# Gate logits of four query chunks in one PSUM bank, spread over the partitions through DRAM: a change to a kernel that mixes two attention blocks

## The chip, the cores and the metric

One core of one Trainium2 chip. The metric is the device time of one execution in microseconds (us). "Span" is the time from the first to the last instruction in a profiled execution; it is some 2 us (up to 3) shorter than the device time of the same run. Engines: PE multiplies, with PEld for its weight loads; ACT is ScalarE, DVE VectorE, POOL GpSimd; SP only issues transfers.

## The reference

Two blocks read 2048 rows of 512 columns and a gate mixes them, row by row:

```python
x = A_x                                                     # [1, 2048, 512] bf16
g = sigmoid((x * gate_w).sum(-1, keepdims=True))            # one number per row
a = softmax attention(x), 32 heads of width 16, then @ A_wo
b = linear attention(x) with phi(t) = t + 1 or exp(t), then @ B_wo
return g * a + (1 - g) * b
```

## The kernel before

The kernel holds a **planner**: tasks are generators that yield steps, each with an engine, an estimated duration and an instruction. The planner picks, time step by time step, what each engine does next, and writes one fixed order of instructions per engine. On the chip every engine runs its own list in order and waits on semaphores. A few dozen constants steer the choices.

The score units (128 keys x 512 queries of one head) have two ways to their exponential: in pairs on ACT, or one at a time on DVE by integer arithmetic on the bits of a bf16, with two shifted copies that DVE or POOL makes. A unit on DVE costs PE three products instead of one. 2048 units are shared out by the planner.

```python
    SWITCH = 100.0
    FILL = 0.7
    HOT = 32.85
    BACK = 980.186
    # ... some forty such constants
    PKR, MTR, PQR, PQS, FR = 0.404, 8.73, 13.55, 1.600, 0.0
    KR, KS, QR = 5.59, 1.48, 4.00

        # matmul on four column tiles of 32, all with the same moving operand
        def mmt(o, l, r, start=True, stop=True):
            def go():
                for j in range(4):
                    h = nc.tensor.matmul(o[32 * j:32 * j + 32], lhsT=l[:, 32 * j:32 * j + 32], rhs=r, start=start, stop=stop,
                                         skip_group_check=True)
                return h
            return go

        def t_v(t8, vb):
            # ... project V, then copy it out of PSUM on DVE:
            yield dv(607, lambda: nc.vector.tensor_copy(Vc[:, 0, vs, :, :, 0:16], src), [r_bank[b]], [r_V[vs]])
            yield ("FREE", b)
            for k in range(1, NTERM):       # two scaled copies of V on POOL, for the units on DVE
                yield po(690, lambda k=k: nc.gpsimd.tensor_scalar(Vc[:, k, vs].rearrange("p a b c -> p (a b c)"),
                                                                  Vc[:, 0, vs].rearrange("p a b c -> p (a b c)"), COEF[k], 1.0,
                                                                  op0=ALU.mult, op1=ALU.mult), [r_V[vs]], [r_V[vs]])

        def t_gate():                       # abridged: see the diff
            # weights copied to 4 x 128 columns on POOL; per chunk of 512 queries: 16 matmuls into a bank of its own,
            # one DVE transpose, one POOL copy of 16 columns; then exp, + 1, reciprocal, 1 - g, four loads of gnat

        def aout(r):                        # after a round of attention; gt is g, natural layout
            # ...
            gv = gt[:, qc, :].unsqueeze(1).to_broadcast([128, n, 16])
            yield dv(155 + 17 * n, lambda: nc.vector.reciprocal(rc, src[:, :, :, 16]), rT1, rr)
            yield po(230 + 25 * n, lambda: nc.gpsimd.tensor_tensor(rgc, rc, gv, ALU.mult), [*rr, r_gt], rrg)
```

The softmax here doesn't subtract the row's maximum and nothing guards it: scores larger than these inputs give would overflow.

## Time and profile before

| | before |
|---|---|
| device time, median of three | 675.63 us |
| span of the profiled run | 674.2 us |
| ACT busy / idle | 658.3 / 15.9 us |
| exponentials of 128x1024 on ACT | 695 (1390 units) |
| units on DVE | 658 |
| ACT idle at the start and end | 9.7 us before 40 us, 6.05 us after 660 us |

In the profile's lines of groups, the columns are line, engine, operation, destination and source, shapes and count, then busy us and mean ns, then the engine's idle time just before them and what ended it. In a time line they are start, length, instruction, and idle time before it in square brackets. The prediction below shows the lines of before.

### The profile page before, as it was taken

The numbers are of one execution on the slowest core, as the hardware profiler recorded it, in microseconds if no ns is written. First come the engines' busy times: TensorE is split into PE (matmuls) and PEld (weight loads), VectorE is DVE, ScalarE is ACT, GpSimd is POOL, SyncE is SP. The second block draws the span as 40 slices with busy tenths as digits, with TensorE's granted clock in tenths as the row PEclk, the third lists the DMA queues.
The fourth block names the chain that finished last, engine by engine and source line by source line (L and its number), as shares of the span: only waits on it lengthen the run. The fifth ranks groups of instructions, "written<-read, shape, count | busy, mean of one in ns | idle before, by whom it ended". The sixth has DMA issues, their size and how long they took to land.

```text
span 674.2 us, 23975 instructions
## 1 busy us (share of the span) xinstructions
PE 660.7 (98%) x9813; PEld 202.2 (30%) x9839; DVE 603.4 (89%) x1053; ACT 658.3 (98%) x735; POOL 559.4 (83%) x617
## 2 busy tenths in 40 slices
PE   8999999999999999999999999999999999999998
PEld 3322323232322232323333322232232332222222
DVE  6999989988888889989999888999899998899985
ACT  6899999999999999999999999999999999999996
POOL 3789888888978888888888888878888989887881
PEclk9999999999999999999999999999999999999999
DMA  6420001200000000000001000001010020000001
GB/s 133 135 84 11 6 1 36 70 10 2 3 10 1 10 2 3 10 2 11 4 2 45 30 10 1 8 12 30 6 34 10 18 42 25 24 19 11 26 17 33
DMA packets 28155, 15.96 MB, mean 24 GB/s; under 512 B 19984, under 2 KB 27024, under 8 KB 28048
## 3 DMA queue, kind: packets, MB, share of 16 engines
q1 hardware_dynamic: 26704, 13.92, 8.2%
q8 instruction: 79, 1.29, 0.8%
q10 hardware_dynamic: 1344, 0.52, 0.3%
q14 instruction: 28, 0.23, 0.1%
HBM read 6.69 MB, written 2.10 MB: 13 GB/s over the span
## 4 chain that ended last, share of the span: by engine, by line
PE 50%; ACT 31%; issue 12%; SPq 2%; DVE 2%; POOL 1%; DMA 1%; ACTq 0%; DVEq 0%; POOLq 0%
PE ps L377 39%; ACT P L778 30%; PE ps L383 10%; SPq L354 2%; DVE Z L692 1%; ACT eb L1083 1%; POOL Z L746 1%; DMA gwc<-in_gate_w_dram 1%; DVE Z L756 0%; POOL Vc L995 0%; SPq L358 0%; ACTq L1495 0%; DVE OAT L1059 0%; DVE wA L1176 0%; DVE T L1031 0%
## 5 line engine op out<-in xcount | busy, mean ns | idle before, releaser
L778 ACT ACTIVATE P<-ps 128x1024 bf16<-128x1024 f32 x695 | 645.5, 1117 | 3.9 <-PE ps L377 3.7
L746 POOL TENSOR_TENSOR Z<-Z,mcon 128x512 int32<-128x512 int32 x471 | 488.0, 1061 | 64.4 <-DVE Z L692 50.4
L692 DVE TENSOR_SCALAR Z<-ps 128x512 int16<-128x512 f32 x658 | 440.4, 683 | 57.2 <-PE ps L377 50.9
L377 PE MATMUL ps<-Qz,KT 32*128 32x512 bf16 x2048 | 271.8, 384 | 3.9 <-ACT P L778 1.7
L377 PE MATMUL ps<-Z,Vc 128*17 128x512 bf16 x1974 | 272.5, 382 | 0.5 <-DVE Z L756 0.3
L377 PE MATMUL ps<-P,Vc 128*17 128x512 bf16 x1390 | 245.0, 383 | 1.0 <-POOL Vc L995 1.0
L377 PEld LDWEIGHTS ps<-Qz,KT 32*128 32x128 bf16 x2048 | 67.8, 91 | 262.7 <-ACT P L778 228.7
L377 PEld LDWEIGHTS ps<-Z,Vc 128*17 128x17 bf16 x1974 | 60.9, 88 | 69.1 <-issue 44.2
L756 DVE TENSOR_SCALAR Z<-Z 128x1024 int16<-128x1024 int16 x187 | 77.3, 433 | 0.0
L377 PEld LDWEIGHTS ps<-P,Vc 128*17 128x17 bf16 x1390 | 55.5, 88 | 60.1 <-issue 46.0
L377 PE MATMUL ps<-warm 128*32 128x512 bf16 (+16 forms) x529 | 55.9, 326 | 4.7 <-issue 2.4
L383 PE MATMUL ps<-xT,wA 128*32 128x512 bf16 (+1 forms) x528 | 43.4, 376 | 0.0
L1084 POOL TENSOR_SCALAR eb<-eb 128x512 f32<-128x512 f32 x32 | 21.0, 656 | 18.7 <-DVE Z L756 10.1
L995 POOL TENSOR_SCALAR Vc<-Vc 128x576 bf16<-128x576 bf16 x32 | 21.7, 679 | 6.0 <-DVE Vc L992 2.3
L377 PEld LDWEIGHTS ps<-warm 128*32 128x32 bf16 (+1 forms) x555 | 19.4, 96 | 18.4 <-issue 10.3
L383 PE MATMUL ps<-wA,OAT 128*32 128x512 bf16 x256 | 23.0, 382 | 0.1
L1071 POOL TENSOR_TENSOR T<-T,rg 128x256 bf16<-128x256 f32 x31 | 19.6, 631 | 4.1 <-PE ps L377 1.0
L1083 ACT ACTIVATE eb<-ps 128x512 f32<-128x512 f32 x32 | 22.7, 709 | 0.0
L383 PE MATMUL ps<-xT,wB 128*32 128x512 bf16 x256 | 22.3, 382 | 0.0
L383 PE MATMUL ps<-wA,xnat 128*32 128x512 bf16 x256 | 22.3, 381 | 0.0
L1035 DVE STREAM_TRANSPOSE T<-ps 128x512 f32<-128x512 f32 x31 | 21.9, 706 | 0.1
L1085 DVE SCALAR_TENSOR_TENSOR phiK<-ps,eb 128x512 bf16<-128x512 f32 x32 | 21.7, 678 | 0.2 <-POOL eb L1084 0.2
(81 smaller groups left out, 276.1 us busy)
## 6 DMA issues: line engine op xcount, KB each, us to landing
Qz<-QT SPq DMA_DIRECT2D x120, 16.0 KB, 1.8
wA<-in_A_wqkv_dram SPq DMA_DIRECT2D x4, 384.0 KB, 4.3
wB<-in_B_wqkv_dram SPq DMA_DIRECT2D x4, 384.0 KB, 3.0
xnat<-in_A_x_dram SPq DMA_DIRECT2D x3, 512.0 KB, 3.8
out_dram<-outt SPq DMA_DIRECT2D x12, 128.0 KB, 1.7
wA<-in_A_wo_dram SPq DMA_DIRECT2D x1, 512.0 KB, 4.6
wA<-in_B_wo_dram SPq DMA_DIRECT2D x1, 512.0 KB, 6.5
out_dram<-wA SPq DMA_DIRECT2D x4, 128.0 KB, 1.7
```

The lines of the kernel that those rows point to most:

```text
L377: return lambda: nc.tensor.matmul(o, lhsT=l, rhs=r, start=start, stop=stop, skip_group_check=sg)
L383: h = nc.tensor.matmul(o[32 * j:32 * j + 32], lhsT=l[:, 32 * j:32 * j + 32], rhs=r, start=start, stop=stop, skip_group_check=True)
L692: return C(DV, OPP, 533 * n + 74, lambda: nc.vector.tensor_scalar(o, i, ZB, 0.0, op0=ALU.add, op1=ALU.max), [r_bank[b] for b in bks], r_Z[ ...
L746: return C(PO, 400, 70 + 484 * n, lambda: nc.gpsimd.tensor_tensor(Z[:, z, 0:512 * n].bitcast(I32), Z[:, z0, 0:512 * n].bitcast(I32), mcon[ ...
L756: return C(DV, 450 if hot else 300, 69 + 134 * n, lambda: nc.vector.tensor_scalar(Z[:, z, 0:512 * n], Z[:, z0, 0:512 * n], float(m), None, ...
L778: return C(AC, 500, 427 * n + 49, lambda: nc.scalar.activation(P[:, slot, 0:512 * n], bank(b0, n), ACT.Exp, scale=ESC), [r_bank[b0 + k] fo ...
L995: yield po(690, lambda k=k: nc.gpsimd.tensor_scalar(Vc[:, k, vs].rearrange("p a b c -> p (a b c)"), Vc[:, 0, vs].rearrange("p a b c -> p ( ...
L1035: yield dv(607, lambda: nc.vector.transpose(T1[:, a, :], bank(7)), [r_bank[7]], [r_T1[a]])
L1071: yield po(640, lambda k=k: nc.gpsimd.tensor_tensor(dst_[:, k], src[:, k, :, 0:16], rgc[:, k].unsqueeze(2).to_broadcast([128, 16, 16]), AL ...
L1083: yield ac(480, lambda: nc.scalar.activation(eb[:, i, :], bank(b), ACT.Exp), [r_bank[b]], [r_eb[i]])
L1084: yield po(640, lambda: nc.gpsimd.tensor_scalar(eb[:, i, :], eb[:, i, :], 1.0 + 1e-6, 0.0, op0=ALU.min, op1=ALU.max), [r_eb[i]], [r_eb[i]])
L1085: yield dv(607, lambda: nc.vector.scalar_tensor_tensor(dst_ap, bank(b), 1e-6, eb[:, i, :], op0=ALU.max, op1=ALU.add), [r_bank[b], r_eb[i]] ...
```

## The change

The four chunks' logits go into one bank, one chunk per column tile, with 32 weight columns instead of 128. One transpose then gives all logits, but with the chunks in different partition quarters. The sigmoid is taken on 16 columns. To have every quarter see all chunks, the result is stored to a DRAM buffer of 8 KB and loaded four times, once per quarter, into gt, which holds g for the first block; gnat, loaded from it by way of POOL, holds 1 - g for the second. The diff also sets twelve of the planner's constants anew.

```diff
-    HOT = 32.85
-    BACK = 980.186
+    HOT = 45.668
+    BACK = 977.283
     ... and PLATE, SLK, AGE, PEP, HOLD, BIAS, TTOL, MTR, PQS, KR
         def t_gate():
-            yield po(900, lambda: nc.gpsimd.tensor_copy(gwr, gwc[:].unsqueeze(2).to_broadcast([128, NCC, 128])), [r_gw], [r_gwr])
-            yield ("WAIT", lambda: ("x", 0) in flags and phi_free[0])
-            phi_free[0] = False
-            for qc in range(NQC):
-                b = yield ("BANK",)
-                for h in range(2):
-                    yield pe_step(2, 512, [mmt(bank(b), gwr[:, cc, :], xT[:, cc, 512 * qc:512 * (qc + 1)], ...)
-                                           for cc in (2 * h, 2 * h + 1)], ...)
-                yield dv(607, lambda b=b: nc.vector.transpose(gl, bank(b)), [r_bank[b]], [r_gl, *r_outt])
-                yield ("FREE", b)
-                yield po(250, lambda qc=qc: nc.gpsimd.tensor_copy(ge[:, qc, :], gl.rearrange("p (a b) -> p a b", b=32)[:, :, 0]), ...)
-            ... exp, + 1, reciprocal, 1 - g on 64 columns; four loads of gnat
+            yield po(400, lambda: nc.gpsimd.tensor_copy(gwr, gwc[:].unsqueeze(2).to_broadcast([128, NCC, 32])), [r_gw], [r_gwr])
+            yield ("WAIT", lambda: all(("x", t) in flags for t in range(NQC)))
+            b = yield ("BANK",)
+            def g4(cc):
+                def go():
+                    for j in range(4):
+                        h = nc.tensor.matmul(bank(b)[32 * j:32 * j + 32], lhsT=gwr[:, cc, :], rhs=xT[:, cc, 512 * j:512 * (j + 1)], ...)
+                    return h
+                return go
+            for h in range(2):
+                yield pe_step(2, 512, [g4(2 * h), g4(2 * h + 1)], ...)
+            yield dv(607, lambda: nc.vector.transpose(gl, bank(b)), [r_bank[b]], [r_gl, *r_outt])
+            yield ("FREE", b)
+            ... exp on ACT, + 1 on POOL, reciprocal on DVE, 16 columns each
+            yield ("DMA", scr, ge[:, 0, :], semGN, 16, 2500.0, [r_ge], [r_scr], False, True)
+            for a in range(4):
+                yield ("DMA", gt[32 * a:32 * (a + 1), :, :], scr.rearrange("(q i) b -> i q b", q=NQC), semGT, 64, ...)
+            yield po(200, lambda: nc.gpsimd.tensor_scalar(gp[:], gt[:].rearrange("p q (c a) -> p a (q c)", a=4), -1.0, 1.0, ...),
+                     [r_gt], [r_gp])
+            ... four loads of gnat from gp
             yield ("FLAG", lambda: flags.add("gate"))
```

More of the change, by code (lines that the diff above doesn't have):

```diff
@@ L164, in bass_gated_mix__mha_block__linear_attn_block__prompt_kernel @@
     PMIN = 2
-    PLATE = -199.667
-    SLK = 88.975
+    PLATE = -168.321
+    SLK = 146.603
     DSL = 843.776
@@ L171, in bass_gated_mix__mha_block__linear_attn_block__prompt_kernel @@
     DENS = 0.743
-    AGE = 300.0
-    PEP = 148.771
+    AGE = 140.993
+    PEP = 147.128
     PVD = 216
@@ L176, in bass_gated_mix__mha_block__linear_attn_block__prompt_kernel @@
     MZD = 0.0
-    HOLD = 109.508
+    HOLD = 16.447
     NACT = 4
-    BIAS = 82.599
+    BIAS = 65.881
     KEYW = 7.061
@@ L182, in bass_gated_mix__mha_block__linear_attn_block__prompt_kernel @@
     DTOL = 186.116
-    TTOL = 37.928
-    PKR, MTR, PQR, PQS, FR = 0.404, 8.73, 13.55, 1.600, 0.0
-    KR, KS, QR = 5.59, 1.48, 4.00
+    TTOL = 64.585
+    PKR, MTR, PQR, PQS, FR = 0.404, 8.00, 13.55, 1.835, 0.0
+    KR, KS, QR = 6.02, 1.48, 4.00
     NB = 2
@@ L231, in bass_gated_mix__mha_block__linear_attn_block__prompt_kernel @@
         T2 = SB([128, 2, 512], BF16, "T2")
-        gwr = T2[:, 0, :].rearrange("p (c n) -> p c n", c=NCC)
+        gwr = T2[:, 0, 0:128].rearrange("p (c n) -> p c n", c=NCC)
         OAT = SB([128, NT8, S], BF16, "OAT")
@@ L242, in bass_gated_mix__mha_block__linear_attn_block__prompt_kernel @@
         gt = SB([128, NQC, 16], FP32, "gt")
-        ge = SB([128, NQC, 16], FP32, "ge")
+        ge = SB([128, 2, 16], FP32, "ge")
+        gp = SB([128, 4, 16], FP32, "gp")
+        scr = nc.dram_tensor("gate_rows", [128, 16], FP32).ap()
         gnat = SB([128, NKB], FP32, "gnat")
@@ L288, in bass_gated_mix__mha_block__linear_attn_block__prompt_kernel @@
         r_mcon = R("mcon")
-        r_gt, r_ge, r_gl, r_gnat = R("gt"), R("ge"), R("gl"), R("gnat")
+        r_gt, r_ge, r_gl, r_gp, r_gnat, r_scr = R("gt"), R("ge"), R("gl"), R("gp"), R("gnat"), R("scr")
         r_OBT = [R(f"OBT{i}") for i in range(NKB)]
@@ L399, in bass_gated_mix__mha_block__linear_attn_block__prompt_kernel @@
         semGN = SEM("s_gn")
+        semGP = SEM("s_gp")
+        semGT = SEM("s_gt")
         semOB = [SEM(f"s_ob{i}") for i in range(2)]
@@ L1000, in t_gate @@
         def t_gate():
-            yield po(900, lambda: nc.gpsimd.tensor_copy(gwr, gwc[:].unsqueeze(2).to_broadcast([128, NCC, 128])), [r_gw], [r_gwr])
-            yield ("WAIT", lambda: ("x", 0) in flags and phi_free[0])
-            phi_free[0] = False
-            for qc in range(NQC):
-                b = yield ("BANK",)
-                for h in range(2):
-                    yield pe_step(2, 512, [mmt(bank(b), gwr[:, cc, :], xT[:, cc, 512 * qc:512 * (qc + 1)], start=(cc == 0), stop=(cc == NCC - 1))
-                                           for cc in (2 * h, 2 * h + 1)], [r_xT[qc][h], r_gwr], [r_bank[b]])
-                yield dv(607, lambda b=b: nc.vector.transpose(gl, bank(b)), [r_bank[b]], [r_gl, *r_outt])
-                yield ("FREE", b)
-                yield po(250, lambda qc=qc: nc.gpsimd.tensor_copy(ge[:, qc, :], gl.rearrange("p (a b) -> p a b", b=32)[:, :, 0]),
-                         [r_gl, *r_outt], [r_ge])
@@ L1013, in t_gate @@
-            phi_free[0] = True
-            yield ac(300, lambda: nc.scalar.activation(gt[:], ge[:], ACT.Exp, scale=-1.0), [r_ge], [r_gt])
-            yield po(200, lambda: nc.gpsimd.tensor_scalar(ge[:], gt[:], 1.0, None, op0=ALU.add), [r_gt], [r_ge])
-            yield dv(650, lambda: nc.vector.reciprocal(gt[:], ge[:]), [r_ge], [r_gt])
-            gp = ge[:].rearrange("p q c -> p (q c)")
-            yield po(200, lambda: nc.gpsimd.tensor_scalar(gp.rearrange("p (a u) -> p a u", a=4), gt[:].rearrange("p q (c a) -> p a (q c)", a=4),
-                                                          -1.0, 1.0, op0=ALU.mult, op1=ALU.add), [r_gt], [r_ge])
@@ L1020, in t_gate @@
-            for a in range(4):
-                yield ("DMA", gnat[32 * a:32 * (a + 1), :], gp[32 * a:32 * (a + 1), 16 * a:16 * (a + 1)], semGN, 64, 2500.0, [r_ge], [r_gnat], False, a == 0)
+            yield po(400, lambda: nc.gpsimd.tensor_copy(gwr, gwc[:].unsqueeze(2).to_broadcast([128, NCC, 32])), [r_gw], [r_gwr])
[4 more added lines that the diff above has]
+                    for j in range(4):
+                        h = nc.tensor.matmul(bank(b)[32 * j:32 * j + 32], lhsT=gwr[:, cc, :], rhs=xT[:, cc, 512 * j:512 * (j + 1)],
+                                             start=(cc == 0), stop=(cc == NCC - 1), skip_group_check=True)
+                    return h
+                return go
@@ new lines, in t_gate @@
+            for h in range(2):
+                yield pe_step(2, 512, [g4(2 * h), g4(2 * h + 1)], [*[r_xT[t][h] for t in range(NQC)], r_gwr], [r_bank[b]])
+            yield dv(607, lambda: nc.vector.transpose(gl, bank(b)), [r_bank[b]], [r_gl, *r_outt])
+            yield ("FREE", b)
+            yield ac(230, lambda: nc.scalar.activation(ge[:, 0, :], gl.rearrange("p (a b) -> p a b", b=32)[:, :, 0], ACT.Exp, scale=-1.0),
+                     [r_gl, *r_outt], [r_ge])
+            yield po(150, lambda: nc.gpsimd.tensor_scalar(ge[:, 1, :], ge[:, 0, :], 1.0, None, op0=ALU.add), [r_ge], [r_ge])
@@ new lines, in t_gate @@
+            yield dv(170, lambda: nc.vector.reciprocal(ge[:, 0, :], ge[:, 1, :]), [r_ge], [r_ge])
+            yield ("DMA", scr, ge[:, 0, :], semGN, 16, 2500.0, [r_ge], [r_scr], False, True)
+            for a in range(4):
+                yield ("DMA", gt[32 * a:32 * (a + 1), :, :], scr.rearrange("(q i) b -> i q b", q=NQC), semGT, 64, 2800.0, [r_scr], [r_gt], False, a == 0)
+            yield po(200, lambda: nc.gpsimd.tensor_scalar(gp[:], gt[:].rearrange("p q (c a) -> p a (q c)", a=4), -1.0, 1.0, op0=ALU.mult, op1=ALU.add),
+                     [r_gt], [r_gp])
@@ L1022, in t_gate @@
+            for a in range(4):
+                yield ("DMA", gnat[32 * a:32 * (a + 1), :], gp[32 * a:32 * (a + 1), a, :], semGP, 64, 2500.0, [r_gp], [r_gnat], False, a == 0)
             yield ("FLAG", lambda: flags.add("gate"))
```

## The prediction

> **What bounds the kernel now.** I read the page's engine table first, then the chain that ended last, then the costliest groups, then the windows, then the waits of ACT, and last the time line around the one large hole that they showed.
>
> ```profile
> PE 660.7 (98%) x9813; PEld 202.2 (30%) x9839; DVE 603.4 (89%) x1053; ACT 658.3 (98%) x735; POOL 559.4 (83%) x617
> PE 50%; ACT 31%; issue 12%; SPq 2%; DVE 2%; POOL 1%; DMA 1%; ACTq 0%; DVEq 0%; POOLq 0%
> ...
> L778 ACT ACTIVATE P<-ps 128x1024 bf16<-128x1024 f32 x695 | 645.5, 1117 | 3.9 <-PE ps L377 3.7
> L746 POOL TENSOR_TENSOR Z<-Z,mcon 128x512 int32<-128x512 int32 x471 | 488.0, 1061 | 64.4 <-DVE Z L692 50.4
> L692 DVE TENSOR_SCALAR Z<-ps 128x512 int16<-128x512 f32 x658 | 440.4, 683 | 57.2 <-PE ps L377 50.9
> ...
> L756 DVE TENSOR_SCALAR Z<-Z 128x1024 int16<-128x1024 int16 x187 | 77.3, 433 | 0.0
> L377 PE MATMUL ps<-warm 128*32 128x512 bf16 (+16 forms) x529 | 55.9, 326 | 4.7 <-issue 2.4
> ```
>
> Two engines show 98%. PE's figure is flattered: 55.9 us of it are matmuls on the tile warm, which feed nothing and stand where PE would have waited. ACT's is real work, the exponentials of the softmax. The chain alternates between the two because every exponential waits for scores and every score pair waits for a free bank. So I ask where ACT itself is idle:
>
> ```profile
> 0.00:20.00 20.00, 18.05 (x268) 7.74 (x269) 14.28 (x26) 13.56 (x16) 9.44 (x32) 1.00 0.61 126
> 20.00:40.00 20.00, 18.86 (x377) 6.89 (x375) 17.97 (x31) 16.71 (x19) 16.02 (x20) 1.00 0.41 124
> 40.00:660.00 620.00, 612.70 (x9024) 183.84 (x9044) 563.92 (x979) 619.89 (x693) 533.01 (x567) 1.00 0.07 17
> 660.00:674.20 14.20, 11.04 (x161) 3.68 (x153) 7.19 (x20) 8.15 (x11) 0.96 (x1) 1.00 0.11 38
> ```
>
> The columns are stretch, length, then busy time of PE, PEld, DVE, ACT and POOL, clock, DMA share and GB/s. ACT is idle 6.4 us at the start, 3.3 us from 20 to 40, 0.1 us over the next 620 us, and 6.05 us at the end: 15.9 us, which with 658.3 busy makes the span of 674.2. Between 40 and 660 us the kernel is ACT's queue and nothing else. Only two things can shorten it: fewer exponentials on ACT, or smaller holes at the ends.
>
> The largest hole, 2.48 us, has a history that the time line tells, one engine after the other (ACT, POOL, PE):
>
> ```profile
> 21.54 1.02 ACT L778 ACTIVATE P<-ps 128x1024 bf16<-128x1024 f32 x1 [0.21 <-PE ps L377]
> 25.05 1.02 ACT L778 ACTIVATE P<-ps 128x1024 bf16<-128x1024 f32 x1 [2.48 <-PE ps L377]
> ...
> 20.00 1.15 POOL L746 TENSOR_TENSOR Z<-Z,mcon 128x512 int32<-128x512 int32 x1 [0.34 <-DVE Z L692]
> 22.38 0.61 POOL L1001 COPY T<-gwc 128x512 bf16<-128x512 bf16 x1 [1.23 <-DMA gwc<-in_gate_w_dram]
> 23.07 1.47 POOL L995 TENSOR_SCALAR Vc<-Vc 128x576 bf16<-128x576 bf16 x2
> ...
> 24.60 0.40 PE L377 MATMUL ps<-P,Vc 128*17 128x512 bf16 x4 [0.98 <-POOL Vc L995]
> ```
>
> POOL's queue is in order. The gate's copy of the weights (L1001) waits 1.23 us for its load, runs 0.61 us, and only then come the two scaled copies of V, for which PE's next product waits; behind that product stand the scores that ACT wants. So a piece of the gate is on the path once, at 22 us. The rest of it lies between 30.5 and 59 us, beside a busy ACT.
>
> **What the Trainium skill says.** "TensorEngine Tiling (Array Packing)", Key Properties: different tiles can load weights and multiply in parallel. The trace agrees: four gate matmuls on four column tiles take 0.39 us, eight 0.61, twelve 0.83, so 0.22 us for each further four. Four products of P and Vc, which stream four different operands, also take 0.40, so giving each tile its own query chunk should cost nothing. "DMA: Bandwidth & Descriptors", Anatomy of one DMA: a small DMA costs about 2 us fixed, mostly the receipt of the write, longest when the target is HBM, and semaphore waits happen on the issuing sequencer. The trace has 1.7 us for the 2 KB pieces of gnat and 1.8 for Qz; no run here yet shows a small store that is read back. "VectorE: DVE Perf Modes", The three transpose paths: the DVE transpose works on 32x32 blocks. That is why 32 equal columns of logits per chunk suffice, and the trace times one bank at 0.706 us.
>
> **The change, part by part.** PE: 64 matmuls, 16 rounds of four, become 16, four rounds; 12 x 0.22 = 2.6 us less. They can displace matmuls on warm, so alone this is worth about nothing. DVE: four transposes become one, 3 x 0.706 = 2.1 us less; the reciprocal shrinks from 64 to 16 columns, where the trace has 0.553 at 64, 0.334 at 32 and 0.204 at 8 columns, so about 0.25 (estimate), 0.3 less. Sum 2.4 us. POOL: four copies of 0.202 go (0.8); the weight copy falls from 512 to 128 columns, 0.61 to about 0.3 (estimate, from 0.20 for 16 columns and 0.30 for 64); the addition falls from 0.38 to about 0.2. Sum 1.3 us. ACT: the one exponential goes from 0.315 to about 0.25, under 0.1 us. Three other PSUM bank occupations of the gate go too.
>
> Added: one store of 8 KB and four loads of 8 KB through DRAM, in front of the four loads of gnat that stay. The four issues of gnat took 2.41 us; so issue and landing of the store about 0.6 + 2.0, of the loads 2.4 + 1.8, then POOL 0.3: the gate table gt is ready some 7 us after the reciprocal (estimate). gt is first needed by L1069, at 58.6 us. The one matmul step needs all of x, whose last transposing load was issued at 16.97 us and lands about 3 us later, so it can run by 25 to 35 us; with 2 us for transpose, exponential, addition and reciprocal gt is there by 45 us at the latest. Slack over 10 us: the round trip is hidden.
>
> What is on the path: the weight copy in front of V, 0.3 us shorter; the wait for its load stays unless the order changes. The freed DVE and POOL time is worth something only where the static schedule turns it into score units taken off ACT. There are 695 x 2 + 658 = 2048 units. A unit on DVE costs (440.4 + 77.3) / 658 = 0.79 us there plus 488.0 / 658 = 0.74 us of POOL; on ACT it costs 645.5 / 1390 = 0.46 us. DVE's 2.4 us buy three units, which is 1.4 us of ACT; POOL's 1.3 us and its idle 17% can follow. Sum: 0.3 + 1.4 + 0.1 = 1.8 us, if all is collected.
>
> The diff also retunes some fifteen constants of the scheduler that lays out the static order. They decide how eagerly DVE takes units, when POOL takes shifts and when the second block's projections begin. I cannot compute their effect; it reorders nearly every instruction. New values were presumably picked because they do well with the smaller gate, so I expect 0 to 4 us of gain, centred near 1. A stretch where ACT lost 0.1 us in 620 leaves them little but the share of units and the two ends.
>
> **Rivals.** (1) The wait moves. The SP queue is in order, and the store waits for the reciprocal, the loads for the store, the gnat loads for POOL. If the gate comes at 32 us, the eight Qz loads of the second pair, issued at 35.62 before, queue behind some 7 us. The first exponential was at 9.31 and a round of 64 units lasts about 620 / 2048 x 64 = 19 to 20 us, so those Qz are needed near 49 us; landing moves from about 43 to 50. For it: everything shares one queue. Against: the scheduler knows these waits and SP idles long otherwise. It would cost 1 to 2 us of ACT once: 674 to 676. (2) The hole at 22 us closes. With another order, V's copies would follow the shift that ended at 21.15, 1.9 us sooner than 23.07, and ACT would get most of 2.48 us back: with the 1.8 above some 671.5 to 672. For it: the new order is drawn afresh; against: the copy is still the gate's first step with the same release. (3) Nothing is collected: the 2.4 us of DVE become idle time, as 50.9 us of waiting for PE before L692 already are, and the time stays at 675 to 676. (4) The retuning finds a better split, say ten units more off ACT, 4.6 us: 669 to 671. DVE at 89% and POOL at 83% leave room, the matmuls on warm too.
>
> **Range and chances.** Direct effects -1.8 us if collected, taken at two thirds: -1.2; retuning -1; the hole at 22 us -0.7 as a weighted chance; queueing on SP +0.2. Together -2.7 us from 675.6, so 673.0. The three runs before spread 1.5 us, and a reordered schedule may move 2 to 3 us either way; the low side is wider because constants are usually kept when they help. Range 668.5 to 676.5. Two per cent is 13.5 us, nearly all of ACT's idle time, or 29 units; faster than that 0.03, slower 0.02, within 0.95.
>
> **What would show it.** In the changed profile: 16 matmuls on xT and the gate weights, one transpose, no copy to ge; ACT near 657 us with 692 to 694 exponentials, and D units 662 to 664; ACT idle under 0.5 us from 40 to 650; gt read by L1069's counterpart without a wait on a DMA. Rival 1 shows as PE or POOL waiting for a DMA of Qz or gt between 40 and 60 us; rival 2 as ACT's idle time from 20 to 40 us falling from 3.3 to about 1; rival 3 as 695 exponentials again; rival 4 as 690 or fewer. The prediction is wrong if the count of exponentials moves by more than five, or if either end of the kernel changes by more than 3 us.

## The result

673.93 us (median of four, 673.4 to 674.5) against 675.77 us for the kernel before in the same rounds (675.01 to 676.53): ratio 0.9973, interval 0.9956 to 0.9990, within 2%, output correct. A ratio here is the mean time of one kernel's fast runs over that of the other's of the same rounds, so not quite the ratio of the medians.

The changed kernel's groups, with the same columns as before:

```profile
PE 663.6 (99%) x9796; PEld 200.4 (30%) x9796; DVE 600.1 (89%) x1053; ACT 657.3 (98%) x734; POOL 560.5 (83%) x614
...
L782 ACT ACTIVATE P<-ps 128x1024 bf16<-128x1024 f32 x694 | 644.6, 1123 | 2.3 <-PE ps L379 2.2
...
L696 DVE TENSOR_SCALAR Z<-ps 128x512 int16<-128x512 f32 x660 | 441.2, 682 | 56.3 <-PE ps L379 51.1
...
L379 PE MATMUL ps<-warm 128*32 128x512 bf16 (+15 forms) x556 | 66.6, 331 | 1.2 <-DVE dummy L431 1.2
```

Two units, one pair, went from ACT to DVE. The filler matmuls on the tile warm read 55.9 us before and 66.6 us now, but that is the trace and not the change: the trace of before lacks 26 records of matmuls (PE x9813 against PEld x9839 in the prediction's first line), all of them fillers, and this one lacks none. A second profile of the changed kernel, which lacks 32, reads 57.6 us. Counted by their weight loads there are 555 fillers before and 556 now. Two stretches of the windows (columns as in the prediction):

```profile
20.00:40.00 20.00, 19.77 (x378) 7.01 (x375) 17.16 (x31) 18.19 (x21) 17.56 (x21) 1.00 0.41 127
40.00:658.00 618.00, 615.28 (x9009) 182.04 (x9006) 562.07 (x980) 618.00 (x690) 532.99 (x562) 1.00 0.07 17
```

The time line at the hole, first ACT's, then POOL's:

```profile
23.80 8.80 ACT L782 ACTIVATE P<-ps 128x1024 bf16<-128x1024 f32 x9 [1.09 <-PE ps L379]
```

```profile
21.88 1.42 POOL L999 TENSOR_SCALAR Vc<-Vc 128x576 bf16<-128x576 bf16 x2
23.36 0.29 POOL L1005 COPY T<-gwc 128x128 bf16<-128x128 bf16 x1
```

The copy of the gate weights now stands behind the copies of V, and the hole at 22 us is 1.09 us instead of 2.48. ACT idles 1.81 us from 20 to 40 us instead of 3.29, and not at all from 40 to 658 us.

The span fell by 2.3 us: 1.0 us less ACT work (one exponential 0.9, the gate's own exponential 0.09) and 1.3 us less ACT idle time (6.58 + 1.81 + 6.21 = 14.6 us). So both gains that the prediction named, fewer exponentials and the hole, are there. What the profile cannot say is whether the smaller gate or the redrawn order brought them. The experiments ask that.

### The profile page after: what moved, and what is told of

The parts are those of the page before. It is cut to its first block, busy times and chain, and to the rows that moved or that the text cites. A ratio compares the mean times of both kernels' runs of the same rounds, so it can differ in the third digit from the quotient of the medians.

```text
span 671.9 us, 23950 instructions
## 1 busy us (share of the span) xinstructions
PE 663.6 (99%) x9796; PEld 200.4 (30%) x9796; DVE 600.1 (89%) x1053; ACT 657.3 (98%) x734; POOL 560.5 (83%) x614
## 4 chain that ended last, share of the span: by engine, by line
PE 61%; ACT 27%; issue 9%; DVE 2%; POOL 1%; ACTq 0%; POOLq 0%
PE ps L379 47%; ACT P L782 25%; PE ps L385 13%; ACT eb L1092 1%; POOL Z L750 1%; DVE Z L696 1%; POOL Vc L999 0%; DVE Z L760 0%; PE ps L910 0%; PE ps L1012 0%; ACTq L1504 0%; DVE OAT L1068 0%; DVE T L1040 0%; DVE Vc L996 0%; DVE T L1065 0%
## 5 line engine op out<-in xcount | busy, mean ns | idle before, releaser
L379 PE MATMUL ps<-P,Vc 128*17 128x512 bf16 x1388 | 241.9, 383 | 0.1
L379 PEld LDWEIGHTS ps<-P,Vc 128*17 128x17 bf16 x1388 | 54.0, 88 | 57.9 <-issue 45.0
L379 PE MATMUL ps<-warm 128*32 128x512 bf16 (+15 forms) x556 | 66.6, 331 | 1.2 <-DVE dummy L431 1.2
L385 PE MATMUL ps<-phiK,xnat 128*32 128x512 bf16 x256 | 21.9, 381 | 0.0
```

Of the source, the lines that this page charges most:

```text
L379: return lambda: nc.tensor.matmul(o, lhsT=l, rhs=r, start=start, stop=stop, skip_group_check=sg)
```

## The experiments

Twelve runs, five rounds each (six for three_more_hops) beside the kernel before on the same chip; three chips were used, so ratios are compared, not times. "Plan" is the order that the planner lays out. "ACT waits" is the time in which an exponential waited for scores, in the profiled run; "tail" runs from the end of the last exponential to the end of the span.

| run | gate | plan | ratio to before (interval) | median us | exponentials | ACT waits | tail |
|---|---|---|---|---|---|---|---|
| before | old | own | 1 | 675.8 to 676.5 | 695 | 3.7 | 7.7 |
| changed kernel, again | new | own | 0.9972 (0.9960 to 0.9984) | 673.71 | 694 | 2.3 | 7.7 |
| old_gate_new_constants | old | the other's constants | 1.0050 (1.0036 to 1.0063) | 679.37 | 697 | 4.0 | 9.4 |
| new_gate_old_constants | new | the other's constants | 1.0058 (1.0046 to 1.0071) | 679.80 | 695 | 4.0 | 10.4 |
| gate_work_removed | 1/4 of old | kept | 1.0001 (0.9988 to 1.0013) | 676.20 | 695 | 4.2 | 7.7 |
| copy_after_v | old | kept, one move | 0.9997 (0.9984 to 1.0009) | 675.68 | 695 | 2.9 | 7.7 |
| old_gate_replanned | old | redrawn | 0.9978 (0.9966 to 0.9991) | 674.16 | 693 | 5.9 | 7.8 |
| old_gate_replanned_2 | old | redrawn | 0.9985 (0.9971 to 0.9999) | 675.29 | 694 | 4.8 | 7.7 |
| new_gate_replanned | new | redrawn | 0.9991 (0.9979 to 1.0003) | 675.54 | 693 | 4.6 | 8.3 |
| new_gate_replanned_2 | new | redrawn | 0.9973 (0.9960 to 0.9985) | 674.57 | 694 | 3.4 | 7.6 |
| old_gate_replanned_copy_late | old | redrawn, one move | 0.9968 (0.9955 to 0.9980) | 673.97 | 693 | 2.9 | 7.7 |
| three_more_hops | new | kept | 1.0071 (1.0058 to 1.0085) | 681.21 | 694 | 9.6 | 7.9 |
| three_more_hops_late_reader | new | kept, one move | 0.9964 (0.9951 to 0.9976) | 673.45 | 694 | 2.3 | 7.7 |

Not in the table is the moment of the first exponential, 8.56 to 10.11 us in these profiles. It varies by itself: in the four profiles that share the changed kernel's start it is 9.04 to 9.53 us. Spans of single profiles compare no better than that.

The first theory (A) was that the smaller gate itself brings the gain; the rivals were that the constants do (B), or only a plan that fits its gate (C).

### The two halves of the change: old_gate_new_constants and new_gate_old_constants

```diff
 # old_gate_new_constants: the kernel before with
-    HOT = 32.85
+    HOT = 45.668
 # ... and the eleven other constants of the changed kernel (the text on record miscounts them as sixteen)
 # new_gate_old_constants: the changed kernel with the twelve constants of before
```

> The kernel before with only the sixteen planner constants of the changed kernel (its gate as it was). Theory A (the gain of 1.8 us is the smaller gate's own: the hole at 22 us and two units moved to DVE): the constants alone do nothing, 675.0 to 676.5 us, exponentials 694 to 696. Theory B (the gain is the retuning's): 673.5 to 674.5 us with about 694 exponentials. Theory C (the constants only fit the plan that they were tuned with, so that gate and constants pay only together): slower than before, 677 to 680 us, with more exponentials on ACT, about 697, which the static program already has; each is 0.93 us of ACT.

> The changed kernel with the constants of before. Theory A: the gate alone keeps the gain, 673.5 to 674.5 us. Theory B: the gate alone gives at most its hole at 22 us, 674.5 to 675.7 us. Theory C: slower than before in spite of less work, 677 to 680 us; the static program has 695 exponentials, as before, so the loss would have to show as idle time of ACT between 20 us and the end, over 17 us in sum where before has 15.9.

Both were slower than the kernel before, by 0.50% and 0.58%. With the new gate the exponentials are those of before (695) although the gate is smaller. The loss is at the end. This view gives the window after the last exponential, counting only instructions that touch the output weights (first kernel: before; second: new_gate_old_constants):

```profile
666.49:674.20 7.71, 4.54 (x75) 1.78 (x72) 0.69 (x1) 1.66 (x3) 0.00 (x0) 1.00 0.21 70
```

```profile
667.08:677.50 10.42, 7.61 (x133) 3.48 (x132) 0.69 (x1) 1.75 (x3) 0.00 (x0) 1.00 0.20 65
```

After its last exponential, before has 75 matmuls of output blocks to do, the crossed kernel 133: some two blocks of 32 matmuls that a fitting plan hides among the exponentials stand behind them, and the tail is 2.7 us longer. In old_gate_new_constants it is 104 matmuls and two more exponentials; its profiled run is the slowest of its five, 1.9 us above their median, and started its exponentials 0.8 us later than before.

The hole at 22 us, on the other hand, closes with the old gate too once it has the new constants. Its copy, still of 512 columns, stands behind V's copies, and ACT waits 1.09 us as in the changed kernel (POOL, then ACT):

```profile
24.02 0.61 POOL L1001 COPY T<-gwc 128x512 bf16<-128x512 bf16 x1
```

```profile
24.46 1.94 ACT L778 ACTIVATE P<-ps 128x1024 bf16<-128x1024 f32 x2 [1.09 <-PE ps L377]
```

So that piece can be had from the order without the smaller gate, and it does not decide the time: this kernel is the slower one. Neither half of the change pays alone, as theory C had it: the constants fit one list of tasks.

### The gate's work taken out, nothing moved: gate_work_removed

The plan was laid out with the old gate's steps, but three chunks' instructions were left out when the order was written. Its output is wrong, which doesn't matter for the time.

```diff
-                    yield pe_step(2, 512, [mmt(...) for cc in (2 * h, 2 * h + 1)], ...)
+                    yield pe_step(2, 512, [mmt(...) if qc == 3 else None for cc in (2 * h, 2 * h + 1)], ...)
-                yield dv(607, lambda b=b: nc.vector.transpose(gl, bank(b)), ...)
+                yield dv(607, (lambda b=b: nc.vector.transpose(gl, bank(b))) if qc == 3 else None, ...)
                 # the POOL copy likewise: at qc == 3 only, and to all 64 columns
 # None: the step takes its planned time, no instruction is written
```

> The kernel before with its order kept, but the matmuls, transposes and copies of three of the four gate chunks left out (wrong on purpose: all four query chunks get the gate of the last one). It takes 2.6 us of PE, 2.1 us of DVE and 0.6 us of POOL away between 30 and 54 us and moves nothing. If freed time of PE, DVE and POOL is worth nothing until the plan moves units with it: within 0.3 us of before. If it is worth something by itself: up to 1.8 us less, and ACT's idle time between 20 and 60 us falls.

Ratio 1.0001. In the window from 20 to 60 us (first before, second this run) PE is busy 2.66 us less and DVE 1.99 us less, and ACT does not gain from it. It is even 0.47 us less busy, chiefly because POOL waited 1.73 us for the load of the gate weights instead of 1.23, so that the hole at 22 us was 3.17 us in this run:

```profile
20.00:60.00 40.00, 38.86 (x637) 12.28 (x635) 36.88 (x65) 36.71 (x42) 32.64 (x41) 1.00 0.29 88
```

```profile
20.00:60.00 40.00, 36.20 (x584) 11.30 (x573) 34.89 (x61) 36.24 (x42) 32.10 (x38) 1.00 0.28 89
```

Time freed on PE, DVE and POOL is worth nothing here while the order stays as it is.

### The hole at 22 us alone: copy_after_v

```diff
-            yield po(900, lambda: nc.gpsimd.tensor_copy(gwr, gwc[:]...), [r_gw], [r_gwr])
+            yield po(900, None, [r_gw], [r_gwr])           # keeps its place in the plan, writes nothing
 # in t_v: the instruction goes in front of the first scaled copy of the next V block
+                if (t8, vb, k) == (0, 2, 1):
+                    yield po(690, [gcopy, vmul], [r_V[vs], r_gw], [r_V[vs], r_gwr])
```

> The kernel before with its order of instructions kept on every engine but for one move: the copy of the gate weights on POOL is issued behind the two scaled copies of V that it stood in front of. If the hole of 2.48 us in ACT at 22 us comes from that copy and its load, POOL starts the V copies at 21.2 instead of 23.07 us, ACT's idle time from 20 to 40 us falls from 3.3 to about 1.5 us and the span by 1.5 to 1.9 us, since ACT is never idle afterwards: ratio 0.9972 to 0.9978. If another wait takes its place (PE or DVE late as well), under 0.5 us.

POOL's time line in this run:

```profile
22.02 1.42 POOL L1003 TENSOR_SCALAR Vc<-Vc 128x576 bf16<-128x576 bf16 x2 [0.39 <-DVE Vc L1000]
26.35 0.61 POOL L1007 COPY T<-gwc 128x512 bf16<-128x512 bf16 x1 [2.91 <-DVE Vc L1000]
```

Measured from the first exponential (9.31 us in before, 9.79 here), the copies of V start 1.53 us sooner, after a wait of 0.39 us for another producer: DVE's cast of V out of PSUM (L1000). ACT's hole is 1.43 us, 1.05 less:

```profile
24.48 4.88 ACT L786 ACTIVATE P<-ps 128x1024 bf16<-128x1024 f32 x5 [1.43 <-PE ps L385]
```

Some of this comes back: ACT's other holes up to 40 us grow from 0.72 to 0.97 us in sum, which leaves 0.8 us. The moved copy now stands in front of the next V copies; that it causes this is not shown. In the timed runs even the 0.8 us is not clear (0.9997, give or take 0.0013, which is 0.8 us). The expectation of 1.5 to 1.9 us failed, and its other branch, another wait and under 0.5 us, fits: the hole had a second wait close behind the first.

### Does the gain need the new gate? The replanned kernels

The planner's constants were drawn anew for both gates by searches of one kind and size: by the author's account, random steps over 21 constants, about 1,030 plans each, ranked by the end time that the planner itself expects. There were two searches per gate, one from each kernel's constants. PEP, the planner's figure for PE's latency, was left alone. Three of the four edits look like this, and the gate code is untouched in all:

```diff
 # old_gate_replanned                   # old_gate_replanned_2                # new_gate_replanned
-    HOT = 32.85                       -    HOT = 32.85                       -    HOT = 45.668
+    HOT = 49.39                       +    HOT = 40.015                      +    HOT = 44.835
 # ... BACK, PLATE, SLK, ...            # ... BACK, PLATE, SLK, ...            # ... PLATE, DSL, AGE, ...
```

> The changed kernel as it is, on the chip and in the rounds of the next three: ratio 0.996 to 0.999 to before, 673.4 to 675 us.

> The kernel before with its gate untouched; only the planner's constants are drawn anew, by a search of the same kind and size for old and new gate over the order that the planner lays out (started from the constants of the changed kernel). The static program has 693 exponentials and 662 units on DVE, where before has 695 and 658. Theory A (the gain needs the smaller gate): no better than before, 675.5 to 677 us, since each redrawn plan of the old gate pays the gate's work. Theory C (the gain is that of a well fitting plan; the smaller gate gives at most about 1 us of it): 673 to 674.7 us, a ratio of 0.996 to 0.9985, with ACT busy some 1.8 us less than in before.

> The changed kernel with its constants drawn anew by the same search. 693 exponentials, one less than in the changed kernel. Theory C: 672 to 673.5 us, about 1 us below the old gate replanned, which is what the 2.4 us of DVE and 1.3 us of POOL are worth when a fitting plan is found for both. Theory A: 671 to 672.5 us, and 3 us or more below the old gate replanned.

> The kernel before, its gate untouched, with a second plan of its own, from a search that started at its own constants: 694 exponentials, 661 units on DVE. Theory C (the plan decides, the gate's size hardly): 674 to 676.5 us, so that old and new gate overlap over their plans. Theory A (each plan of the old gate pays its work): 675.5 us or more, as the first replanned one was the exception.

> The changed kernel with a second new plan, from a search that started at the constants of before: 694 exponentials, 660 units on DVE, as in the changed kernel. Theory C: 673.5 to 676 us, in the same range as the replanned old gate. Theory A: below 673.5 us and clearly below both replanned old gates.

The old gate with a redrawn plan gave 0.9978 and 0.9985, the new gate with three plans 0.9972, 0.9991 and 0.9973. The intervals overlap. That is theory C: a gain of the change's size can be had without touching the gate. The changed kernel itself, run again in these rounds, repeated its result (673.71 us). Redrawing the new gate's plan gave nothing more: new_gate_replanned has one exponential less than the changed kernel and lost it in waits (4.6 against 2.3 us) and in the tail (8.3 against 7.7). At 675.54 us it missed both branches of its expectation. A few tenths of a microsecond for the new gate are not excluded; these runs cannot settle that.

The first replanned old gate has a weakness that the profile shows, its five runs going from 673.85 to 677.42 us. The profiled run is the 677.42, and its span of 674.5 us stands against 672.1 to 672.5 us for the other four. POOL's time line, ACT's, and one stretch of the windows:

```profile
22.90 0.61 POOL L1001 COPY T<-gwc 128x512 bf16<-128x512 bf16 x1 [1.98 <-DMA gwc<-in_gate_w_dram]
```

```profile
25.62 1.02 ACT L778 ACTIVATE P<-ps 128x1024 bf16<-128x1024 f32 x1 [3.28 <-PE ps L377]
```

```profile
26.00:29.00 3.00, 3.00 (x68) 1.50 (x64) 1.04 (x3) 1.91 (x3) 0.84 (x2) 0.52 0.03 5
```

POOL waits 1.98 us for the weights' load, ACT stands for 3.28 us, and behind it PE's granted clock is 0.52 of full from 26 to 29 us, while its matmuls in that stretch take up to 0.64 us where most take 0.39. So I gave this plan the one move of copy_after_v.

### A version to beat both: old_gate_replanned_copy_late

The edit is the two of copy_after_v and old_gate_replanned together.

> The first replanned old gate, its order kept but for the one move tried before: the copy of the gate weights behind the two scaled copies of V. There POOL waited 1.98 us for the load of the weights and ACT stood for 3.28 us in the profiled run, against 2.48 us in before. The move took about 1 us off the hole in before, of which some 0.8 us remained at 40 us. Expected: 0.7 to 1.5 us below the first replanned old gate, 672.8 to 673.6 us, a ratio of 0.9958 to 0.997, and so as fast as the changed kernel or a little faster, without its gate; if the hole is nothing but a shift of the same wait, equal to the first replanned old gate within 0.3 us.

673.97 us, ratio 0.9968. The hole is 1.43 us again, and ACT waits 2.9 us in sum. The ratio is where it was expected, but it differs from old_gate_replanned's 0.9978 by less than either interval, and it does not beat the changed kernel (0.9972) beyond noise. Within noise it equals it, with the old gate.

### How much slack has the round trip? three_more_hops and three_more_hops_late_reader

```diff
 # three_more_hops: in front of the first load of gt, on the same queue, order otherwise kept
+                for k in range(3):      # each waits for the one before it
+                    eng.dma_start(scrs[k + 1], scrs[k])
 # three_more_hops_late_reader: besides, the POOL step 1 - g and the loads of gnat go from 47 us to the fourth round
-            yield po(200, lambda: nc.gpsimd.tensor_scalar(gp[:], gt[:]..., -1.0, 1.0, ...), [r_gt], [r_gp])
+            yield po(200, None, [r_gt], [r_gp])
+            if r == 3:                  # in aout
+                yield po(230 + 25 * n, [gpf, rgf], [*rr, r_gt], [*rrg, r_gp])
```

> The changed kernel, its order kept, with three more copies from DRAM to DRAM in a chain between the store of the gate rows and their loads. The round trip becomes some 7 to 9 us longer. If it is hidden with over 10 us of slack, as the prediction has it: within 0.5 us of the changed kernel. Against it: in the changed kernel POOL's reader of the loads starts at 47.0 us, about 1 us after they land, and POOL's queue is in order, so POOL stands still some 7 us from 47 us on, and the later shifts, the products of P and Z and at last ACT with it: then 1 to 5 us slower, with ACT idle between 45 and 65 us.

> The changed kernel with the three more hops that cost 7.3 us, and with the one POOL instruction that forms 1 minus the gate, with the four loads behind it, moved from 47 us to about 97 us in the order; all else kept. If those 7.3 us come from POOL's in-order queue waiting at that reader: the next reader of the gate table is at 57.6 us, the table is there at 53.2 us, so the loss vanishes, 673.4 to 674.7 us, as the changed kernel. If they come from the SP queue, which the hops hold up (loads of Qz and of the second weights behind them): 679 us or more, as with the hops alone.

Three hops cost 681.21 - 673.71 = 7.5 us against the changed kernel of the same rounds, where 1 to 5 us were expected if POOL stands still. The waits of the profiled run between 45 and 60 us (waiter, releaser: us in total, times, longest), then the time line of POOL and of ACT at the spot:

```profile
ACT P L793 <- PE ps L389: 6.4, 2, 5.5
...
POOL gp L1038 <- DMA gt<-gate_rows: 5.5, 1, 5.5
PE ps L389 <- POOL Z L761: 5.2, 1, 5.2
```

```profile
53.20 0.29 POOL L1038 TENSOR_SCALAR gp<-gt 128x64 f32<-128x64 f32 x1 [5.53 <-DMA gt<-gate_rows]
```

```profile
56.75 2.10 ACT L793 ACTIVATE P<-ps 128x1024 bf16<-128x1024 f32 x2 [5.54 <-PE ps L389]
```

Read upwards from POOL: its queue is in order and stops at the reader of gt, PE waits for the shift behind it, ACT for the scores behind PE. A value that nobody needs before the second block's denominators (1 - g) stopped the kernel's bound engine for 5.5 us. Late in PE's wait of 5.2 us and behind it the granted clock was 0.50 (54 to 58 us), then 0.63 (58 to 60 us), and ACT waited 0.87 us more. A further 1.00 us of the 9.6 us of waits is not the hops': it lies at 28 us, before the first hop was issued (41.46 us), behind a pause of 1.18 us on PE for which the profile shows no wait.

In the changed kernel SP issues the loads of gt, and POOL reads them without a wait:

```profile
41.06 2.74 SPq L360 DMA_DIRECT2D gt<-gate_rows  x4
```

```profile
47.01 0.29 POOL L1027 TENSOR_SCALAR gp<-gt 128x64 f32<-128x64 f32 x1
```

The last of the loads, issued at 43.4 us, landed 1.7 us later, at 45.1 us. So the slack of the round trip was 1.9 us (also in the second profile of the changed kernel), and not the "about 1 us" of the text on record.

With the reader moved to 97.1 us and the same three hops, the loss was gone: 673.45 us, ratio 0.9964, ACT's waits 2.3 us. The SP queue, held up just as long (the loads of gt from 48.72 us), cost nothing.

## Why the prediction was right, and where its reasons were not

- **The time and the class** held: 673.0 predicted, 673.93 measured; a gain of 2.7 us predicted, 1.84 measured in the same rounds.
- **What bounds the kernel** held. ACT is the queue, and what sets the twelve runs apart is its own account: when its exponentials start, how many there are, its waits, and the tail after the last one.
- **PE's 2.6 us worth nothing alone** held, and it is just as true of the 2.1 us of DVE's three transposes (gate_work_removed, 1.0001).
- **The direct effects of 1.8 us, taken at two thirds** are the step that failed. "DVE's 2.4 us buy three units, which is 1.4 us of ACT" was read as the gate's own gain. The changed kernel did move two units (0.93 us). But the old gate with a redrawn plan moved three to four (661 and 662 units on DVE), so what the plan collects is not tied to what the gate frees; and with the constants of before, the new gate collected none and lost 0.58%.
- **Retuning "0 to 4 us of gain, centred near 1"** was mis-sized, and it was wrong to add it to the gate's term as if each stood alone. With the new gate, the new constants are worth 0.86% (1.0058 to 0.9972), some 5.8 us; with the old gate they cost 0.50%. Turned round, the smaller gate is worth 0.78% under the new constants (1.0050 to 0.9972) and costs 0.58% under the old ones. So the crossed runs give neither term a size of its own. That the gain needs no smaller gate is shown by the redrawn old gate alone. That the sum came near is luck in its parts.
- **The hole at 22 us** was read rightly as a piece of the gate on the path. Its closing, held open as rival 2, is what the trace of the changed kernel shows (2.48 to 1.09 us, about 1.4 us), and the redrawn order brings it with the old gate too. Rival 2 did not foresee a further wait: DVE's cast of V, 0.39 us behind in copy_after_v. Moved alone the copy gave no clear gain. It is "the largest hole" only between the first exponential and 660 us: at the end ACT waits 2.69 us once, for the output blocks.
- **"Slack over 10 us: the round trip is hidden"**: hidden, yes; the slack was 1.9 us. I looked for the first reader whose result matters (57.6 us), not for the first reader in an in-order queue (47.0 us). And gt was there 11.1 us after the reciprocal, not 7: on SP's queue five loads of Qz and one of wB stood between the store and the loads of gt (36.35 to 41.0 us).
- **Rival 1, queueing on SP**, did not occur: Qz of the second pair was issued from 33.81 to 40.4 us, before the loads of gt, and ACT did not wait between 40 and 60 us.
- **Counts**: 694 exponentials were inside the predicted 692 to 694, 660 units on DVE outside 662 to 664.

What stays open: how much the smaller gate is worth with the best plan for each. Over three fitting plans each, the old gate has 1, 0.9978 and 0.9985, the new one 0.9972, 0.9991 and 0.9973: means of 0.9988 and 0.9979, some 0.6 us apart, which is less than the half width of one interval (about 0.8 us) and than the spread between plans of one gate.

## What to carry to other kernels

Here one engine was busy almost without a gap, and work removed from the others was worth nothing while the order stayed. So a change that comes with new tuning has to be judged against the old code with new tuning too. To find what a piece of code costs, keep the order and leave out its instructions. For a slow value, look at the first reader in any in-order queue, however unimportant that reader is: moving it later took the whole loss of three more transfers away.

## What the Trainium skill lacked or had wrong

- "DMA: Bandwidth & Descriptors", Anatomy of one DMA: describes transfers issued from GpSimd (these are issued from SP), with some 2 us for a small one and HBM as the slowest target. The trace agrees: 1.7 us for a transfer into gnat, which stays on the chip's SBUF, 2.9 us for the 8 KB store to DRAM. The section has no figure for a value stored and read back. Here: 2.9 us for the store, 2.4 us (1.7 to 2.8) for each load of it, and 8.5 us for a chain of three DRAM to DRAM copies of 8 KB (41.46 to 50.00 us, issue included), 2.85 us each.
- "TensorE: Matmul & The Clock Gate", Why this matters for your kernels: warns of idle gaps over about 3 us. The 5.2 us of three_more_hops fit it (a granted clock of 0.50 from 54 to 58 us). In old_gate_replanned the longest gap was 1.78 us, with PE busy 1.23 of the 2 us from 22 us and 0.83 of the 2 us from 24 us, and a granted clock of 0.52 over 3 us followed. In before, with a gap of 0.98 us at the same place, the clock stayed at 1.00. So a shorter gap can do it too, in some executions: the mean clock of the other four runs of old_gate_replanned was 1.00.
- "TensorEngine Tiling (Array Packing)", Key Properties: gives no time for column tiles that stream different operands; the times for packed tiles in "TensorE: Matmul & The Clock Gate", Part 3, do not say whether the operands differ. Here, eight gate matmuls with four different streams took 0.62 us, with one common stream 0.61 to 0.62.
